# Decoding float64 weights on the chip: the magnitude moved from ScalarE to VectorE, the sign written as a 16-bit float, the weights held at 1/256 of their size

## Chip, cores and metric

The kernel runs on one core of one Trainium2 chip. The metric is the time of one execution on the device in microseconds, as the median of the runs. The engines are TensorE (PE, its weight loads PEld), VectorE (DVE), ScalarE (ACT), GpSimd (POOL) and SyncE (SP), whose queue issues most of the DMA transfers. Each engine runs its own instructions in the order in which they were put into its queue, and waits on semaphores for the others.

## What is computed

Attention that keeps only the 32 best keys of every query, and a feed-forward block with an ELU on its result.

```python
# q, k, v: (8, 8, 576, 64) float32;  w_in: (512, 2048), w_out: (2048, 512) float64
scores = scale * np.matmul(q, k.transpose(0, 1, 3, 2))
kth = np.partition(scores, -top_k, axis=-1)[..., -top_k:-top_k + 1]
scores = np.where(scores >= kth, scores, -1000000000.0)
attn = softmax(scores)                     # with 1e-09 added to the sum
x = (attn @ v) as (4608, 512)
h = x @ w_in
g = np.where(h > 0.0, h, np.exp(np.minimum(h, 0.0)) - 1.0)
out = (g @ w_out).astype(np.float32)
```

The two weight matrices arrive in float64. No engine computes in that format here, so the kernel reads them as pairs of 32-bit words and makes float32 numbers of them itself. That is the decoding, and the change is all about it.

## The kernel before

**Attention.** For each of the 8 batches the 576 queries are cut into four tiles of 128 rows and one of 64. One *step* is one tile with two heads (a row `i` = 0 or 1 for each head; the 64-row tile takes four heads in a step). A step multiplies queries and keys on TensorE (`scores`, L301), copies the scores to SBUF on ScalarE (L309), and finds the 32 largest of each row on VectorE: four `MAX8` passes with three `MATCH_REPLACE8` passes between them (`select_row` L320 to L330, later `select` L343 to L355). Then comes `mask`: GpSimd takes the negated 32nd value and the gap to the largest (L368, L370), ScalarE masks with a very steep Prelu (L371) and takes the exponential with its sum (L372). `normalise` (L382 to L389, GpSimd) divides, `turn` (L408, L409) transposes through TensorE and copies back on ScalarE, and `attend` (L434) multiplies with the values.

**Feed-forward.** `ffn_pieces` cuts the work into pieces. `hidden` multiplies with `w_in` (L506) and writes two Relus from PSUM (L516, L519) and an exponential (L521) on ScalarE; `close_gates` puts them together on VectorE (L478). `project` multiplies with `w_out` (L531), copies the result on ScalarE (L540) and stores it. `feed` deals these pieces out between the attention steps by a plan of costs and due steps (`HIDDEN`, `PROJECT`, `due`), so that TensorE has work all the time. A piece is only dealt out when the pieces of weights that it needs count as decoded (`decoded[0]`).

**Decoding.** The weights come in 32 pieces of 128 x 512 float64 numbers, 16 of each matrix, into a pool `raw` of seven buffers (`load_weight`, L153, SyncE). A number is two words, the low one (`lo`) and the high one (`hi`), so all operations of the decoding go over every second word. One call of `hook` runs `decode_piece(i)`: it issues the load of piece i + 3, the first half of the conversion of piece i (`convert_first`), and the second half for piece i - 3 (`convert_last`).

- L174, ScalarE: the top of the low word's mantissa becomes the low bits of a float32 (`Copy` with a scale and a bias).
- L175, ScalarE: the sign of the number, as an 8-bit float +1 or -1, into the top byte of the low word.
- L178, ScalarE: the magnitude of the high word, read as a float32, scaled by a power of two.
- L179, GpSimd: the magnitude is limited from both sides.
- L186, VectorE (three hooks later): the high word is shifted left by three, which turns the 11-bit exponent into an 8-bit one.
- L187, GpSimd: an integer addition of both words gives the float32 weight and adds the sign bit with the exponent's offset that comes with the sign's own exponent.

The hook is called in `select_row` after the third and the fourth `MAX8` of every row, that is four times in each of the first eight steps (`tight`), and three more times in `select`, where the later steps begin.

**What sets the order.** From step 8 on the program stands inside `manual_schedule`: the four compute engines execute what the Python program issues, in that order. In the first eight steps (apart from the very start) the planner of the language orders the instructions of each engine itself, with the order of the program as priority. The SyncE queue is in order throughout.

Of the kernel before, what the change touches and what calls it, by code (L numbers as in the profile page):

```python
# [8 lines left out]
AF = mybir.ActivationFunctionType  # L9
ALU = mybir.AluOpType  # L10
FP32 = mybir.dt.float32
U32 = mybir.dt.uint32
I32 = mybir.dt.int32
FP8 = mybir.dt.float8e4
PSUM = bass.MemoryType.PSUM

TOP_K = 32
# [2 lines left out]
STEEP = 1.0e30  # L20
HIDDEN = {1: 1.1, 2: 1.85, 3: 2.7}
PROJECT = 3.55


class Tile:
# [56 lines left out]
def kernel(  # L82
# [9 lines left out]
    nc = tc.nc  # L92
# [9 lines left out]
    NF = dff // P  # L102
# [3 lines left out]
    scale = 1.0 / float(D) ** 0.5  # L106
# [33 lines left out]
    raw = {}  # L140
# [10 lines left out]
    def load_weight(i):  # L151
        t = rawpool.tile([P, 2 * WN], U32, tag="raw", name="raw")
        nc.sync.dma_start(t[:], weight(i)[0])  # L153
        raw[i] = t

    def parts(t):
        words = t[:].rearrange("p (n w) -> p n w", w=2)
        signs = t[:].bitcast(FP8).rearrange("p (n w) -> p n w", w=8)
        return words[:, :, 0], words[:, :, 1], signs[:, :, 3]

    def convert_first(i):

        lo, hi, sign = parts(raw[i])
        ef, mf = hi.bitcast(FP32), lo.bitcast(FP32)
        nc.scalar.activation(mf, lo, AF.Copy, scale=2.0**-35, bias=2.0**17)  # L174
        nc.scalar.activation(  # L175
            sign, ef, AF.Sign, scale=2.0**64, bias=1.0, saturate=False
        )
        nc.scalar.activation(ef, ef, AF.Abs, scale=2.0**-62)  # L178
        nc.gpsimd.tensor_scalar(  # L179
            ef, ef, (2.0 - 2.0**-3 - 2.0**-23) * 2.0**-46, 2.0**-77, ALU.min, ALU.max  # L180
        )

    def convert_last(i):
        t, dst = raw.pop(i), weight(i)[1]
        lo, hi, sign = parts(t)
        nc.vector.tensor_single_scalar(hi, hi, 3, ALU.logical_shift_left)  # L186
        nc.gpsimd.tensor_tensor(  # L187
            dst.bitcast(I32), hi.bitcast(I32), lo.bitcast(I32), ALU.add
        )
# [15 lines left out]
    def decode_piece(i):  # L205
        if i < 2 * NF:
            if i + 3 < 2 * NF:
                load_weight(i + 3)
            convert_first(i)
        if i > 2:  # L210
            convert_last(i - 3)
            decoded[0] = i - 2
# [205 lines left out]
    def attend(g):  # L418
# [28 lines left out]
        while tiles:  # L447
            blk, lo, parts = tiles[0].block, tiles[0].cols.start, 0
            while tiles and tiles[0].block is blk:
                parts += 1  # L450
                hi = tiles.pop(0).cols.stop
            finish(blk, parts, g.hp, slice(lo, hi), ps[:, c0 : c0 + hi - lo])
            c0 += hi - lo
# [15 lines left out]
    def close_gates(keep=0, upto=None):  # L469

        while gates:
            put, group, dst, n = gates[0]
            if put > place[0] - keep if upto is None else group > upto:
                return
            gates.pop(0)
            nc.vector.scalar_tensor_tensor(  # L478
                out=dst, in0=n, scalar=-1.0, in1=dst, op0=ALU.add, op1=ALU.add
            )  # L480

    def ffn_pieces(blk):
        n_tok = blk.slots * P
        bank = dm // n_tok
        unit = max(2, bank)

        def hidden(f):
            if f == 0 and blk.number == 0:
                g = early.tile([P, NF, P], FP32, tag="g", name="gT")
                blk.gT = [g[:, 0:NG], g[:, NG:NF]]  # L490
            elif f % NG == 0 and blk.number > 0:
                g = late["g"].tile([P, NG, T], FP32, tag="g", name="gT")
                blk.gT.append(g[:])
            if f % unit == 0:
                if len(gates) > 1:
                    close_gates(upto=gates[0][1])
                if blk.number == 0:
                    n = earlyf.tile([P, 4 * P], FP32, tag="n", name="n")
                else:
                    n = late["f"].tile([P, 2 * T], FP32, tag="n", name="n")  # L500
                blk.n = n[:, 0 : unit * n_tok].rearrange("p (f t) -> p f t", f=unit)
            if f % bank == 0:
                ps = ps_f.tile([P, dm], FP32, tag="f", name="hps")
                blk.h = ps[:, 0 : bank * n_tok].rearrange("p (f t) -> p f t", f=bank)
            for i in range(NC):
                nc.tensor.matmul(  # L506
                    blk.h[:, f % bank, :],
                    w_in[:, i, f * P : (f + 1) * P],
                    blk.xT[:, i, 0:n_tok],
                    start=(i == 0),  # L510
                    stop=(i == NC - 1),
                )
            g, end = blk.gT[f // NG], f % NG + 1
            if end % bank == 0:
                n0 = f % unit + 1 - bank
                nc.scalar.activation(  # L516
                    blk.n[:, n0 : n0 + bank, :], blk.h, AF.Relu, scale=-1.0
                )
                nc.scalar.activation(g[:, end - bank : end, 0:n_tok], blk.h, AF.Relu)  # L519
            if end % unit == 0:  # L520
                nc.scalar.activation(blk.n, blk.n, AF.Exp, scale=-1.0)  # L521
                dst = g[:, end - unit : end, 0:n_tok]
                gates.append((place[0], (blk.number, f + 1 - unit), dst, blk.n))

        def project(s, part):
            close_gates(upto=(blk.number, (part + 1) * NF // 4 - 1))
            if part == 0:
                blk.o = ps_f.tile([P, dm], FP32, tag="f", name="ops")
            step = NF // 4
            for f in range(part * step, (part + 1) * step):  # L530
                nc.tensor.matmul(  # L531
                    blk.o[:],
                    blk.gT[f // NG][:, f % NG, s * P : (s + 1) * P],
                    w_out[:, f, :],
                    start=(f == 0),
                    stop=(f == NF - 1),
                )
            if part == 3:
                o = opool.tile([P, dm], FP32, tag="osb", name="osb")
                nc.scalar.copy(o[:], blk.o[:])  # L540
                for t in blk.tiles[s]:
                    p0 = t.cols.start - s * P
                    nc.sync.dma_start(out[t.rows, :], o[p0 : p0 + t.ql, :])

        part = HIDDEN[blk.slots]
        behind = 2 * NF if blk.number else 0
        return [
            (part, max(behind, NC * (f // 4 + 1)), lambda f=f: hidden(f))
            for f in range(NF)
        ] + [  # L550
            (PROJECT, max(behind, NF + (part + 1) * NF // 4),
             lambda s=s, part=part: project(s, part))
            for s in range(blk.slots)
            for part in range(4)
        ]
# [4 lines left out]
    for b in range(B):  # L560
        if b % 2 == 0:
# [5 lines left out]
            for part in division:  # L567
                blk = Block(len(blocks), len(part))
# [4 lines left out]
        for qt in range(J + 1):  # L573
# [8 lines left out]
            t = Tile(b, qt, rows, blk, slice(c0, c0 + n))  # L582
# [6 lines left out]
        for qts in order:  # L589
# [3 lines left out]
            for qt in qts:  # L593
                n = len(steps)
# [3 lines left out]
    for blk in sorted(blocks, key=lambda x: x.ready):  # L598
        due.append((blk.ready, total))
        total += NF * HIDDEN[blk.slots] + 4 * blk.slots * PROJECT  # L600

# [47 lines left out]
    for hp in range(1, NHP):  # L649
        load_v(0, hp)  # L650
    decode += [lambda i=i: decode_piece(i) for i in range(2 * NF + 3)]
    at(0, start_qk, 0, 2)
    at(1, start_qk, 0, 3)
# [93 lines left out]
```

## Time and profile before

| what | value |
|---|---|
| runs | 1667.3, 1667.61, 1669.78 us; median 1667.61 |
| profiled execution | 1667.86 us, its span 1666.1 us |
| busy over the span | PE 1598.7 (96%), DVE 1495.4 (90%), ACT 1164.9 (70%), POOL 630.4 (38%) |
| first and last decoding instruction | first L174 at 8.5 us, last L187 at 148.6 us |
| granted TensorE clock | 0.972 on average; 0.55 from 40 to 80 us, 0.67 from 80 to 120 us, 0.80 from 120 to 160 us, 1.00 from 160 us to 320 us |
| first selection pass on VectorE (L320) | 15.55 us |

In the views that follow, a line of the groups reads: line, engine, operation, written tile <- read tile, shape and type, count | busy us, mean ns of one | idle us of the engine just before them, and what ended the idle time. A line of the timeline begins with its start and its duration in us; the bracket at its end is the engine's idle time before it and who ended that. A line of the waits reads: who waited <- for whom: us in total, times, longest. A line of the stretches gives the length, then busy us and number of instructions of each engine, then the granted TensorE clock as a share of full speed, and DMA. A busy time contains everything between the start and the end of an instruction, also what it waits inside; back to back instructions of one engine overlap a little, so the distance of two starts is often less than a duration.

### The profile page before, as it was taken

Reading aid. Unit: us, or ns where it says so; the run is one execution under the profiler, and the core shown is the slowest. Engines: PE = TensorE matmul, PEld = TensorE weight load, DVE = VectorE, ACT = ScalarE, POOL = GpSimd, SP = SyncE. Lnnn points to the kernel's source line nnn. Section 1 sums busy time; section 2 is a strip of 40 time slices with the busy share of each in tenths; the row PEclk is TensorE's granted clock in tenths of the full one; section 3 lists DMA queues with packets and bytes.
Section 4 is the critical chain, followed back from the end, with each engine's and each line's share of the span. In section 5 each row is a group of like instructions: output and inputs, shape, how many; then the busy total and the mean of one; then the engine's idle time right before and its main releaser. Section 6 shows DMA issues by size and latency. Waiting matters only on the chain.

```text
span 1666.1 us, 26020 instructions
## 1 busy us (share of the span) xinstructions
PE 1598.7 (96%) x8560; PEld 1037.1 (62%) x8560; DVE 1495.4 (90%) x3044; ACT 1164.9 (70%) x2345; POOL 630.4 (38%) x1719
## 2 busy tenths in 40 slices
PE   5588999999999999999999999999999999999999
PEld 3365777657574767656566676755557575755565
DVE  5887999999999999999999999999999999998500
ACT  6997777668686767678667685868758585857521
POOL 2775444333334334333334333333333343332200
PEclk9568999999999999999999999999999999999999
DMA  7540111001100110011100111001200100000000
GB/s 212 169 145 7 23 48 31 7 15 44 48 1 7 44 42 22 1 28 37 42 14 1 49 29 35 1 14 43 50 13 1 28 15 29 7 7 7 7 14 13
DMA packets 101126, 56.21 MB, mean 34 GB/s; under 512 B 84096, under 2 KB 92288, under 8 KB 100992
## 3 DMA queue, kind: packets, MB, share of 16 engines
q1 hardware_dynamic: 99792, 54.26, 11.7%
q8 instruction: 68, 1.11, 0.3%
q14 instruction: 66, 0.54, 0.1%
q10 hardware_dynamic: 1200, 0.30, 0.1%
HBM read 45.09 MB, written 9.44 MB: 33 GB/s over the span
## 4 chain that ended last, share of the span: by engine, by line
PE 68%; DVE 21%; ACT 8%; issue 1%; POOL 1%; SPq 0%; DMA 0%; ACTq 0%; DVEq 0%; POOLq 0%
PE ops L531 25%; PE hps L506 21%; DVE wk L348 9%; PE avps L434 8%; DVE m L355 8%; PE scps L301 7%; PE eps L408 5%; DVE m L343 3%; ACT raw L175 1%; PE qkps L271 1%; DVE gT L478 1%; ACT sc L372 1%; ACT sc L371 1%; ACT et L409 1%; ACT raw L174 1%
## 5 line engine op out<-in xcount | busy, mean ns | idle before, releaser
L355 DVE MAX8 m<-wk 128x8 f32<-128x576 f32 x816 | 573.1, 741 | 0.0
L506 PE MATMUL hps<-xT,w_in 128*128 128x256 f32 (+2 forms) x2432 | 547.5, 374 | 0.1
L531 PE MATMUL ops<-w_out,gT 128*128 128x512 f32 x1152 | 523.4, 599 | 0.0
L506 PEld LDWEIGHTS hps<-xT,w_in 128*128 128x128 f32 x2432 | 405.8, 192 | 97.8 <-issue 24.8
L348 DVE MATCH_REPLACE8 wk<-m,wk 128x576 f32<-128x576 f32 x544 | 398.2, 737 | 0.0
L531 PEld LDWEIGHTS ops<-w_out,gT 128*128 128x128 f32 x1152 | 208.8, 190 | 233.5 <-issue 221.5
L382 POOL TENSOR_SCALAR dene<-den 128x2 f32<-128x2 f32 x144 | 36.4, 253 | 778.3 <-ACT sc L372 777.6
L371 ACT ACTIVATE sc<-sc,neg 128x576 f32<-128x576 f32 x288 | 226.3, 786 | 79.5 <-POOL neg L368 79.5
L372 ACT ACTIVATE sc<-sc,gap 128x576 f32<-128x576 f32 x288 | 223.8, 777 | 25.2
L301 PE MATMUL scps<-kqT 64*128 64x288 f32 (+1 forms) x1280 | 204.6, 443 | 27.9 <-ACT sc L309 15.6
L309 ACT ACTIVATE sc<-scps 128x576 f32<-128x576 f32 x288 | 173.6, 658 | 76.8 <-PE scps L301 76.8
L389 POOL TENSOR_SCALAR sc<-sc,rec 128x576 f32<-128x576 f32 x288 | 221.2, 778 | 14.9
L409 ACT COPY et<-eps 128x512 f32<-128x512 f32 x288 | 166.6, 578 | 58.1 <-PE eps L408 58.0
L408 PEld LDWEIGHTS eps<-ident,sc 128*128 128x128 f32 x1152 | 144.8, 145 | 88.0 <-issue 48.3
L348 DVE MATCH_REPLACE8 wk<-m,sc 128x576 f32<-128x576 f32 x272 | 199.1, 737 | 0.0
L434 PE MATMUL avps<-et,vT 128*64 128x256 f32 (+2 forms) x2080 | 193.3, 329 | 3.0 <-ACT et L409 2.7
L408 PE MATMUL eps<-ident,sc 128*128 128x128 f32 x1152 | 177.2, 280 | 19.2 <-POOL sc L389 17.9
L478 DVE SCALAR_TENSOR_TENSOR gT<-n,gT 128x512 f32<-128x512 f32 (+1 forms) x132 | 99.1, 751 | 103.1 <-ACT n L521 103.1
L343 DVE MAX8 m<-sc 128x8 f32<-128x576 f32 x272 | 190.5, 739 | 0.0
L301 PEld LDWEIGHTS scps<-kqT 64*128 64x128 f32 (+1 forms) x1280 | 109.0, 182 | 99.4 <-issue 44.9
L434 PEld LDWEIGHTS avps<-et,vT 128*64 128x64 f32 x2080 | 123.4, 142 | 76.2 <-issue 25.1
L516 ACT ACTIVATE n<-hps 128x512 f32<-128x512 f32 (+1 forms) x156 | 87.7, 562 | 72.6 <-PE hps L506 71.0
(46 smaller groups left out, 1160.3 us busy)
## 6 DMA issues: line engine op xcount, KB each, us to landing
kin<-in_k_dram SPq DMA_DIRECT2D x64, 128.0 KB, 2.9
raw<-in_moe_w_in_dram SPq DMA_DIRECT2D x16, 512.0 KB, 5.1
vT<-in_v_dram SPq DMA_DIRECT2D x64, 128.0 KB, 2.3
raw<-in_moe_w_out_dram SPq DMA_DIRECT2D x16, 512.0 KB, 3.9
out_dram<-osb SPq DMA_DIRECT2D x32, 256.0 KB, 2.3
qin<-in_q_dram SPq DMA_DIRECT2D x62, 128.0 KB, 2.8
kin<-in_k_dram SPq DMA_DIRECT2D x32, 32.0 KB, 2.6
vT<-in_v_dram SPq DMA_DIRECT2D x64, 16.0 KB, 2.2
```

Source lines behind the costliest of these rows:

```text
L301: nc.tensor.matmul(wide[i][rows, half, 0:HS], kq[part, q0 : q0 + u.t.ql], kq[part, k0 : k0 + HS], start=True, stop=True,)
L343: nc.vector.max(found[i], cur[i])
L348: nc.vector.match_replace(wk[i], found[i], cur[i], TAKEN)
L355: nc.vector.max(found[i], cur[i])
L371: nc.scalar.activation(sc, sc, AF.Prelu, bias=neg[:], alpha=STEEP)
L372: nc.scalar.activation(sc, sc, AF.Exp, bias=gap[:], accum_out=u.den[:, i : i + 1])
L389: nc.gpsimd.tensor_scalar(u.sc[:, i, :], u.sc[:, i, :], rec[:, i : i + 1], 1.0, ALU.mult, ALU.mult)
L408: nc.tensor.transpose(ps[:, c * P : (c + 1) * P], sc[:, c0 : c0 + P], ident[:])
L409: nc.scalar.copy(g.et[:, chunks, u.at, :], ps[:, 0 : n * P].rearrange("p (c q) -> p c q", c=n),)
L434: nc.tensor.matmul(ps[i * D : (i + 1) * D, cols], vt[:, 2 * J + i if c == J else i * J + c, :], w, start=(c == 0), stop=(c == J),)
L506: nc.tensor.matmul(blk.h[:, f % bank, :], w_in[:, i, f * P : (f + 1) * P], blk.xT[:, i, 0:n_tok], start=(i == 0), stop=(i == NC - 1),)
L531: nc.tensor.matmul(blk.o[:], blk.gT[f // NG][:, f % NG, s * P : (s + 1) * P], w_out[:, f, :], start=(f == 0), stop=(f == NF - 1),)
```

## The change

`convert_first` keeps the two ScalarE operations on the low word and on the sign. The sign is now written as a 16-bit float into the upper half of the low word. A new function, `convert_next`, runs one hook later: VectorE clears the sign bit of the high word with an AND, in place of the Abs on ScalarE, and GpSimd limits the magnitude, with other constants. A 16-bit float +1 has other exponent bits in that place than an 8-bit one, by eight steps of the weight's exponent, so the decoded weights are the true ones times 2 to the minus 8; the scales of the Relus that read the first product and of the output copy undo that.

```diff
-FP8 = mybir.dt.float8e4
+FP16 = mybir.dt.float16
...
+WEIGHT = 2.0**-8
...
     def parts(t):
         words = t[:].rearrange("p (n w) -> p n w", w=2)
-        signs = t[:].bitcast(FP8).rearrange("p (n w) -> p n w", w=8)
-        return words[:, :, 0], words[:, :, 1], signs[:, :, 3]
+        signs = t[:].bitcast(FP16).rearrange("p (n w) -> p n w", w=4)
+        return words[:, :, 0], words[:, :, 1], signs[:, :, 1]
...
     def convert_first(i):
         lo, hi, sign = parts(raw[i])
-        ef, mf = hi.bitcast(FP32), lo.bitcast(FP32)
-        nc.scalar.activation(mf, lo, AF.Copy, scale=2.0**-35, bias=2.0**17)
         nc.scalar.activation(
-            sign, ef, AF.Sign, scale=2.0**64, bias=1.0, saturate=False
+            lo.bitcast(FP32), lo, AF.Copy, scale=2.0**-35, bias=2.0**17
         )
-        nc.scalar.activation(ef, ef, AF.Abs, scale=2.0**-62)
+        nc.scalar.activation(
+            sign, hi.bitcast(FP32), AF.Sign, scale=2.0**64, bias=1.0
+        )
+
+    def convert_next(i):
+        hi = parts(raw[i])[1]
+        nc.vector.tensor_single_scalar(hi, hi, 0x7FFFFFFF, ALU.bitwise_and)
         nc.gpsimd.tensor_scalar(
-            ef, ef, (2.0 - 2.0**-3 - 2.0**-23) * 2.0**-46, 2.0**-77, ALU.min, ALU.max
+            hi.bitcast(FP32), hi.bitcast(FP32),
+            (2.0 - 2.0**-3 - 2.0**-23) * 2.0**17, 2.0**-14, ALU.min, ALU.max,
         )
...
             convert_first(i)
+        if 0 < i <= 2 * NF:
+            convert_next(i - 1)
         if i > 2:
             convert_last(i - 3)
             decoded[0] = i - 2
...
                 nc.scalar.activation(
-                    blk.n[:, n0 : n0 + bank, :], blk.h, AF.Relu, scale=-1.0
+                    blk.n[:, n0 : n0 + bank, :], blk.h, AF.Relu, scale=-1.0 / WEIGHT
                 )
-                nc.scalar.activation(g[:, end - bank : end, 0:n_tok], blk.h, AF.Relu)
+                nc.scalar.activation(
+                    g[:, end - bank : end, 0:n_tok], blk.h, AF.Relu, scale=1.0 / WEIGHT
+                )
...
-                nc.scalar.copy(o[:], blk.o[:])
+                nc.scalar.activation(o[:], blk.o[:], AF.Copy, scale=1.0 / WEIGHT)
```

## The prediction

> **What bounds the kernel now.** I read the span in stretches first, then the busy time by operation, the waits of the early stretch, and the timeline of single instructions there. The profiled execution took 1667.86 us (span 1666.1), 0.25 above the median of the three runs, 1667.61; I sum on the profile and take the gain off the median. Columns of the stretches: PE, PEld, DVE, ACT and POOL busy, then clock, DMA share, GB/s.
>
> ```profile
> 38.00:142.00 104.00, 73.74 (x372) 54.50 (x372) 74.58 (x155) 102.27 (x172) 71.39 (x119) 0.63 0.42 133
> ...
> 160.00:800.00 640.00, 626.79 (x3770) 423.57 (x3767) 640.00 (x1310) 470.20 (x972) 247.79 (x714) 0.99 0.11 27
> 800.00:1666.00 866.00, 859.94 (x4269) 536.10 (x4268) 739.89 (x1496) 558.82 (x1143) 289.19 (x829) 1.00 0.07 19
> ```
>
> After 160 us VectorE has no idle time until 800, then TensorE has almost none, and the order is fixed by the program. So an edit to the decoding of weights, which is over by 149 us, moves the end by as much as it moves the start of that dense part: I pass every microsecond through, gain or loss. TensorE does not forbid it: in the early stretch it is busy 73.7 of 104 us, at a granted clock of 0.63. From 38 to 142 us ScalarE is full, 102.3 of 104. Of the decoding alone that stretch holds (DVE, ACT, POOL):
>
> ```profile
> 38.00:142.00 104.00, 12.28 (x27) 66.39 (x86) 48.56 (x53) 0.63 0.42 133
> ```
>
> Two thirds of ScalarE's stage is decoding. VectorE is idle for 104 - 74.6 = 29.4 us of it, and the waits between 37 and 142 us say for whom:
>
> ```profile
> DVE raw L186 <- POOL raw L179: 22.8, 18, 4.0
> ...
> POOL raw L179 <- ACT raw L178: 13.4, 6, 3.9
> ...
> DVE gT L478 <- ACT n L521: 6.0, 2, 3.4
> ```
>
> VectorE's shift waits for GpSimd's limits, which wait for ScalarE's magnitudes. That is a chain with ScalarE at its head.
>
> **What the change takes off ScalarE.** The groups by shape, then one pair of pieces on ScalarE in order of time:
>
> ```profile
> L175 ACT ACTIVATE raw<-raw 128x512 fp8e4<-128x512 f32 x32 | 40.9, 1394 | 0.1
> ...
> L178 ACT ACTIVATE raw<-raw 128x512 f32<-128x512 f32 x32 | 21.0, 714 | 0.1
> ...
> L174 ACT ACTIVATE raw<-raw 128x512 f32<-128x512 uint32 x32 | 20.9, 711 | 5.1 <-DMA raw<-in_moe_w_in_dram 5.1
> ```
>
> ```profile
> 74.65 1.25 ACT L174 ACTIVATE raw<-raw 128x512 f32<-128x512 uint32 x2
> 75.78 2.50 ACT L175 ACTIVATE raw<-raw 128x512 fp8e4<-128x512 f32 x2
> 77.99 1.28 ACT L178 ACTIVATE raw<-raw 128x512 f32<-128x512 f32 x2
> 79.15 0.79 ACT L371 ACTIVATE sc<-sc,neg 128x576 f32<-128x576 f32 x1
> ```
>
> By the starts a piece costs 0.565 (Copy), 1.105 (Sign) and 0.58 us (Abs). Abs goes: 0.58. The sign with 16-bit output is in no row: it lies between 0.565, like the 4-byte outputs beside it in the same strided tile, and 1.105 as now. Less than 0.565 I exclude, since no pass over 512 elements here is cheaper by more than a few hundredths. I take 0.565: only the one-byte output is slow here, and the strides are the same. So 1.12 us a piece, and 29 of 32 pieces are converted after 38 us: 32.5 us, and ScalarE's load falls from 102.3 to 69.8.
>
> The page "ScalarE: Activation LUTs", section "What ACT_TABLE_LOAD costs", in the Trainium skill, gives every function one element per cycle, for fp32 and bf16 alike, with 186 ns + 0.833 ns an element. The sign row above breaks it at 1394 ns, so the rule as printed does not cover one-byte outputs; by it the new sign would last an estimated 613 ns, and the sum would be that of the forecast.
>
> **What it puts on VectorE.** One AND a piece, the form of the shift (uint32 words at the same stride, one constant). An unobstructed shift delays the next VectorE instruction by 0.41 us at most, so 29 x 0.41 = 11.9 us, and VectorE's load in this stage is 74.6 + 11.9 = 86.5. The stage can shorten by 104 - 86.5 = 17.5 us at the utmost. Two things come off that.
>
> First, VectorE and GpSimd block each other:
>
> ```profile
> 59.57 1.04 POOL L187 TENSOR_TENSOR w_in<-raw 128x512 int32<-128x512 int32 x1
> ```
>
> ```profile
> 59.62 1.27 DVE L186 TENSOR_SCALAR raw<-raw 128x512 uint32<-128x512 uint32 x1
> 60.82 0.75 DVE L330 MAX8 m<-wk 128x8 f32<-128x576 f32 x1
> ```
>
> This shift lasted 1.27 instead of 0.41: it ended 0.28 us after GpSimd's add did. Of the 32 shifts 20 had waited for data, mostly for GpSimd itself, and so met it idle or won against it (0.43 us each, the first 0.46). Of the other 12 three met it at work and lost 0.35, 0.86 and 0.35: on average 0.13 us. Once the shifts no longer wait, all 29 shifts and 29 ANDs are of this second kind: 58 x 0.13 = 7.5 us. The bounds are 0 and 58 x 0.52 = 30 (each loses the mean of those three); I take the mean over the 12, the nearest rows.
>
> The Trainium skill speaks here against the change: "SBUF — State Buffer", section "SBUF: two separate sides", says that a VectorE operation in a two-port mode and a GpSimd operation hold one port pair as an exclusive lock for a whole instruction. The row above agrees, but nine of the twelve free shifts were not held up; if all were by it, the sum would be that of the slower rival or worse.
>
> Second, new waits. The AND of piece i-1 stands at hook i in VectorE's in-order queue, ahead of the shift of i-3 and the next selection pass, and waits for ScalarE's Sign of i-1. The distance from conversion to first use on VectorE shrinks from three hooks to one. If Sign is late, the selection stands still, and with it GpSimd's negation and ScalarE's masking. GpSimd's limits go one hook later, past the add of the earlier piece and, for every second piece, past the row's negation and gap (in every second row the normalisation too). The loads on SP keep their places and are freed by the same adds. The price lies between 0 and today's 22.8 us. ScalarE's free time grows from 2% to nearly 30% of the stage, so I keep a fifth: 4.5 us.
>
> Before 38 us the first two pieces stand ahead of the first key copy and the first score copies on ScalarE; the second piece is tied to its load, which lands at 13.0 us, and its sign delays the score copy by 0.54 us less: 0.6 us gained, with bounds 0 and 1.3 (the first piece's Sign and Abs).
>
> **What costs nothing.** The hidden layer's Relu gets other constants: L516 with a scale and L519 without have 595 and 594 ns. The output copy becomes an ACTIVATE with a scale; against 578 ns for a 128x512 COPY from PSUM the ACTIVATE L516 has 595, so 36 x 0.017 = 0.6 us at most, behind 111.9 us of idle time before that line; uncovered, only the last copy's 0.02 us counts.
>
> Sum: 17.5 - 7.5 - 4.5 + 0.6 = 6.1 us. The median goes to 1661.5 us.
>
> **Rivals.** *GpSimd's hold (slower).* In the stage GpSimd is busy 71.4 of 104 us, and of fewer microseconds a larger part, some 0.72. If an AND or shift meets it that often and then loses the 0.52 us mean, the price is 0.72 x 0.52 x 58 = 21.7, and 17.5 - 21.7 - 4.5 + 0.6 = -8.1: 1675.7 us. It decides from (17.5 - 4.5 + 0.6) / 58 = 0.23 us an operation on. For it: the three long shifts, and that GpSimd runs the limits as soon as an AND ends, just when the shift is due. Against it: the nine free ones.
>
> *The sign stays slow (no change).* If 2-byte output is as slow as 1-byte, ScalarE loses only 29 x 0.58 = 16.8 and keeps 85.5 us beside VectorE's 86.5 + 7.5. Two full queues wait for each other more: I keep 40% of 22.8, 9.1, and no early gain. 104 - 94 - 9.1 leaves 0.9: 1666.7 us. For it: nothing in the trace shows a 2-byte output. Against it: the cause may as well be the 8-bit conversion, and I hold that likelier.
>
> *All of the slack is taken (faster still).* With no hold and no new wait 17.5 + 0.6 to 1.3: about 1649 us. It needs two engines without one wait between them.
>
> **How the numbers follow.** A measurement of this kernel tells some 0.2%, 3.3 us, from no change. Forecast 0.43, with its best end another 0.07: faster 0.50. Slow sign, or a forecast whose waits eat all but 3 us: same 0.20. GpSimd's hold, or late signs that act alike: slower 0.30. The order of the first eight steps is the planner's, not written by hand, so it can also change with the edit, in either direction; that keeps me from being surer. The range goes from 1650, a little inside the full slack, to 1677, a little beyond the slower rival; about 2 in 10 stay outside. The likeliest case alone spans 1655 to 1664.
>
> **What would show it.** Right: the sign near 0.7 us mean, no Abs, ScalarE near 70 us between 38 us and the stage's end, VectorE near full there, and its dense part starting about 6 us earlier. Wrong on the sign: still about 1.4 us. Wrong on the hold: ANDs and shifts with means over 0.64 us. Wrong on new waits: an AND that waits for Sign, more than 5 us in all. If the stage shortens and the end doesn't, the pass-through fails: idle time of VectorE between 160 and 800 us would show it.

## The result, and the profile after

The changed kernel takes 1674.3 us (median of six runs, 1671.97 to 1675.98) beside 1667.46 us of the kernel before in the same series. The ratio is 1.0036 with an interval of 1.0026 to 1.0047: slower by 6.8 us, where 6.1 us less had been forecast. The profiled execution took 1671.97 us, its span 1670.1 us. It is the quickest of the six, so the profile shows the loss a little too small.

The stretches, with the columns of the prediction:

```profile
38.00:142.00 104.00, 59.16 (x352) 43.41 (x350) 86.07 (x181) 89.20 (x143) 71.72 (x118) 0.72 0.44 135
160.00:800.00 640.00, 625.55 (x3774) 422.45 (x3773) 640.00 (x1305) 467.95 (x968) 249.09 (x719) 1.00 0.10 27
800.00:1666.00 866.00, 863.81 (x4284) 537.86 (x4282) 743.83 (x1506) 561.17 (x1150) 288.11 (x829) 1.00 0.07 19
```

Again VectorE is without a gap from 160 to 800 us and TensorE nearly so after that. The early stretch now has ScalarE at 89.2 of 104 us instead of 102.3, and VectorE at 86.1 instead of 74.6. Neither is full. The decoding alone (DVE, ACT, POOL), which was 12.28, 66.39 and 48.56:

```profile
38.00:142.00 104.00, 27.19 (x54) 54.53 (x58) 45.23 (x52) 0.72 0.44 135
```

ScalarE lost 12 us of decoding here and VectorE got 15. Beside the decoding VectorE did less in the same 104 us, 58.9 us of work instead of 62.3. The groups by shape, in the order of the answer, say why it is not more:

```profile
L177 ACT ACTIVATE raw<-raw 128x512 f16<-128x512 f32 x32 | 42.1, 1365 | 0.2
...
L183 DVE TENSOR_SCALAR raw<-raw 128x512 uint32<-128x512 uint32 x32 | 18.0, 563 | 26.5 <-ACT raw L177 26.4
...
L192 DVE TENSOR_SCALAR raw<-raw 128x512 uint32<-128x512 uint32 x32 | 14.8, 464 | 5.7 <-POOL raw L184 5.6
```

The first line is the sign: 1365 ns with a 16-bit output, 1394 with an 8-bit one. It did not get faster. L183 is the new AND, with 26.4 us of VectorE's idle time in front of it over the whole span, all of it for the sign. L192 is the shift. ScalarE's pair of pieces now, in order of time:

```profile
77.43 1.24 ACT L174 ACTIVATE raw<-raw 128x512 f32<-128x512 uint32 x2
78.55 2.52 ACT L177 ACTIVATE raw<-raw 128x512 f16<-128x512 f32 x2
80.80 0.75 ACT L379 ACTIVATE sc<-sc,neg 128x576 f32<-128x576 f32 x1
```

By the starts a sign costs (80.80 - 78.55) / 2 = 1.125 us. Abs is gone, the sign is as it was. The waits between 37 and 142 us:

```profile
DVE raw L183 <- ACT raw L177: 12.9, 11, 3.9
...
DVE raw L192 <- POOL raw L184: 4.9, 3, 3.0
```

Before, VectorE's shift had waited 22.8 us for GpSimd's limits. Now the AND waits 12.9 us for the sign and the shift 4.9 us for the limits. The longest of these waits, on all engines in order of time (a bracket holds the idle time before, and who ended it):

```profile
68.65 0.91 POOL L397 TENSOR_SCALAR sc<-sc,rec 128x576 f32<-128x576 f32 x1
...
70.12 0.27 ACT L417 COPY et<-scps 128x128 f32<-128x128 f32 x1 [0.67 <-PE scps L416]
...
71.45 1.22 ACT L174 ACTIVATE raw<-raw 128x512 f32<-128x512 uint32 x2
...
73.23 1.34 ACT L177 ACTIVATE raw<-raw 128x512 f16<-128x512 f32 x1
...
74.61 0.43 DVE L183 TENSOR_SCALAR raw<-raw 128x512 uint32<-128x512 uint32 x1 [3.94 <-ACT raw L177]
...
75.12 0.66 POOL L184 TENSOR_SCALAR raw<-raw 128x512 f32<-128x512 f32 x1 [2.35 <-DVE raw L183]
```

It goes round all engines. GpSimd normalises a row late (L397), after an add of the decoding. TensorE transposes that row late, ScalarE stands in front of the copy of it (L417), and then has the Copies of two pieces (L174) and a masking pass ahead of the first sign. VectorE stands 3.94 us at the AND with the next `MAX8` behind it, and GpSimd's limits (L184) stand 2.35 us for the AND.

The hold between VectorE and GpSimd is there too:

```profile
87.39 1.03 POOL L193 TENSOR_TENSOR w_in<-raw 128x512 int32<-128x512 int32 x1
87.47 1.25 DVE L183 TENSOR_SCALAR raw<-raw 128x512 uint32<-128x512 uint32 x1
```

This AND ended at 88.72, 0.30 us after GpSimd's add. Nine of the 32 ANDs lost time in this way, 4.6 us together, and six shifts 1.5 us.

### The profile page after: what moved, and what is told of

It reads as the page before. It is cut to its first block, busy times and chain, and to the rows that moved or that the text cites. A ratio compares the mean times of both kernels' runs of the same rounds, so it can differ in the third digit from the quotient of the medians.

```text
span 1670.1 us, 26030 instructions
## 1 busy us (share of the span) xinstructions
PE 1585.9 (95%) x8560; PEld 1026.6 (61%) x8560; DVE 1511.5 (91%) x3076; ACT 1148.3 (69%) x2313; POOL 631.0 (38%) x1719
## 4 chain that ended last, share of the span: by engine, by line
PE 69%; DVE 19%; ACT 7%; POOL 2%; issue 2%; SPq 0%; DMA 0%; ACTq 0%; POOLq 0%; DVEq 0%
PE ops L541 24%; PE hps L514 22%; DVE wk L356 8%; PE avps L442 8%; PE scps L309 7%; DVE m L363 7%; PE eps L416 5%; DVE m L351 2%; ACT sc L380 1%; PE qkps L279 1%; ACT sc L379 1%; DVE gT L486 1%; ACT raw L177 1%; PE scps L416 1%; ACT et L417 1%
## 5 line engine op out<-in xcount | busy, mean ns | idle before, releaser
L379 ACT ACTIVATE sc<-sc,neg 128x576 f32<-128x576 f32 x288 | 225.7, 784 | 89.6 <-POOL neg L376 89.5
L397 POOL TENSOR_SCALAR sc<-sc,rec 128x576 f32<-128x576 f32 x288 | 221.5, 779 | 15.0
L309 PE MATMUL scps<-kqT 64*128 64x288 f32 (+1 forms) x1280 | 199.9, 437 | 16.0 <-ACT et L417 5.6
L417 ACT COPY et<-eps 128x512 f32<-128x512 f32 x288 | 166.0, 576 | 62.3 <-PE eps L416 62.3
L442 PE MATMUL avps<-et,vT 128*64 128x256 f32 (+2 forms) x2080 | 189.1, 323 | 4.7 <-ACT et L417 4.5
L442 PEld LDWEIGHTS avps<-et,vT 128*64 128x64 f32 x2080 | 120.0, 139 | 77.4 <-issue 23.9
L309 PEld LDWEIGHTS scps<-kqT 64*128 64x128 f32 (+1 forms) x1280 | 106.6, 180 | 86.1 <-issue 45.4
```

Of the source, the lines that this page charges most:

```text
L309: nc.tensor.matmul(wide[i][rows, half, 0:HS], kq[part, q0 : q0 + u.t.ql], kq[part, k0 : k0 + HS], start=True, stop=True,)
L379: nc.scalar.activation(sc, sc, AF.Prelu, bias=neg[:], alpha=STEEP)
L397: nc.gpsimd.tensor_scalar(u.sc[:, i, :], u.sc[:, i, :], rec[:, i : i + 1], 1.0, ALU.mult, ALU.mult)
L417: nc.scalar.copy(g.et[:, chunks, u.at, :], ps[:, 0 : n * P].rearrange("p (c q) -> p c q", c=n),)
L442: nc.tensor.matmul(ps[i * D : (i + 1) * D, cols], vt[:, 2 * J + i if c == J else i * J + c, :], w, start=(c == 0), stop=(c == J),)
```

## The experiments

Every edit is to the changed kernel. Times are medians; "against before" is the difference to the median of the kernel before in the same series (1668.15, 1668.22 and 1668.08 us in the three series). "Stage" is how much later or earlier than in the kernel before VectorE's selection passes come at the end of step 8 (from 148 us of the kernel before on), in the profiles; "idle" is VectorE's idle time from 38 us to its last shift.

| run | against before, us | ratio and its interval | stage, us | idle, us |
|---|---|---|---|---|
| before | 0 | 1 | 0 | 29.4 |
| the change | +6.8 | 1.0036 (1.0026 to 1.0047) | +3.1 | 17.9 |
| sign16 | +0.7 | 1.0001 (0.9992 to 1.001) | +1.3 | 29.4 |
| and8 | +5.9 | 1.0031 (1.002 to 1.0043) | +6.0 | 21.5 |
| sign32 | -1.7 | 0.999 (0.9981 to 0.9999) | -3.1 | 12.9 |
| nolimits | -14.2 | 0.9916 (0.9903 to 0.993) | -14.0 | 13.1 |
| and_nolim | +1.5 | 1.0008 (0.9998 to 1.0017) | +2.1 | 17.0 |
| and_twice | +14.9 | 1.0086 (1.0073 to 1.01) | +15.3 | 16.7 |
| lag2 | +5.4 | 1.0031 (1.0021 to 1.004) | +4.5 | 17.3 |
| lag2sign32 | -4.8 | 0.9973 (0.9964 to 0.9982) | -4.9 | 9.3 |
| sign32abs | -4.8 | 0.9967 (0.9955 to 0.998) | -5.8 | 22.3 |
| nolow | -12.7 | 0.9923 (0.991 to 0.9935) | -13.9 | 15.3 |
| lean | -16.4 | 0.9894 (0.9881 to 0.9908) | -20.2 | 6.9 |

**Why is the sign slow?** The first run appends ScalarE operations to the end of the kernel, four of each form, all 128 x 512.

```diff
+    bench(halves[:, :, 1], bhi, AF.Sign, **big)
+    bench(quarters[:, :, 3], bhi, AF.Sign, saturate=False, **big)
+    bench(blo, bhi, AF.Sign, **big)
...
+    bench(flat16, flat, AF.Sign, **big)
+    bench(halves[:, :, 1], bhi, AF.Copy)
...
```

> The changed kernel with 56 more ScalarE operations behind its end, four each of fourteen forms over 128x512 elements, on scratch data; its time is longer by these and says nothing. Asked is why the sign takes 1.36 us with 16-bit output. If the narrow output is slow: Sign to dense or strided float32 near 0.7 us, Sign and Copy to the 16-bit and 8-bit places near 1.36. If the write into part of a word is slow: dense 16-bit output near 0.7, strided 1.36. If the function Sign is slow: every Sign near 1.3, Copy and Abs to the same places near 0.7, and Tanh either.

ScalarE's timeline; a line holds the four operations of one form:

```profile
1670.63 5.42 ACT L739 ACTIVATE bench<-bench 128x512 f16<-128x512 f32 x4
...
1676.08 5.43 ACT L739 ACTIVATE bench<-bench 128x512 fp8e4<-128x512 f32 x4
...
1681.55 2.70 ACT L739 ACTIVATE bench<-bench 128x512 f32<-128x512 f32 x4
...
1689.30 2.60 ACT L739 ACTIVATE bench<-bench 128x512 f16<-128x512 f32 x4
```

In order: sign to strided 16 bits, to strided 8 bits, to strided 32 bits, to dense 16 bits. One operation lasts 1335, 1335, 651 and 629 ns. Copy and Tanh with the strided 16-bit output have 1335 as well, Copy to strided 8 bits too, and Copy and Abs to strided 32 bits 651. So neither the function nor the conversion is slow, nor the stride alone, nor 16 bits alone: it is an output narrower than four bytes written with gaps. All the slow rows also read with gaps; a narrow output with gaps from a dense input, and other gaps, were not measured.

The same question inside the kernel: the sign as a 32-bit float over the whole low word. That overwrites what Copy wrote, so the three lowest bits of the weights are lost, but Copy stays for its time.

```diff
-WEIGHT = 2.0**-8
+WEIGHT = 2.0**-1
...
-        return words[:, :, 0], words[:, :, 1], signs[:, :, 1]
+        return words[:, :, 0], words[:, :, 1], words[:, :, 0].bitcast(FP32)
```

> The changed kernel with the sign written as a 32-bit float over the whole low word (weights at one half), so that it takes some 0.65 instead of 1.36 us; the three low bits from the low word are overwritten, and its conversion is kept only for its time. This is what the prediction assumed of the sign. Theory S: the forecast holds, 1658 to 1665, and VectorE waits for the sign less than 6 us. Theory W: the distance of one hook costs all the same, 1668 to 1675, with 10 us of wait or more.

Measured: 1666.52 us in eleven runs, 8.5 us better than the change by the differences to before. The sign's group, and the waits between 37 and 142 us (the line numbers are one lower than in the changed kernel):

```profile
L176 ACT ACTIVATE raw<-raw 128x512 f32<-128x512 f32 x32 | 21.0, 676 | 0.2
```

```profile
DVE raw L182 <- ACT raw L176: 7.5, 4, 3.3
...
DVE raw L191 <- POOL raw L183: 5.9, 3, 3.5
```

With the sign that the forecast had assumed the change is about even, and not 6 us faster: VectorE still idles 12.9 us. That lies between the two expectations: the quick sign is worth a good part of what was missing, and most of the waits stay with it.

**Which half of the change costs?** One keeps the 16-bit sign and the scales, and leaves the magnitude to an Abs on ScalarE, in its old place:

```diff
+        ef = hi.bitcast(FP32)
+        nc.scalar.activation(ef, ef, AF.Abs)
...
-        nc.vector.tensor_single_scalar(hi, hi, 0x7FFFFFFF, ALU.bitwise_and)
...
-            convert_next(i - 1)
```

> The changed kernel with the magnitude back on ScalarE (Abs), in convert_first ahead of GpSimd's limits; 16-bit sign and scaled weights stay. Theory 1 (the loss is the AND on VectorE: its time, the holds against GpSimd and the waits for the sign): as before within 2 us, since the sign costs 1.36 for 1.39 us: 1665 to 1670. Theory 2 (the loss comes with the 16-bit sign and the scales in the later operations): 1671 to 1676, near the changed kernel.

The other keeps the AND, with the 8-bit sign of before:

```diff
-WEIGHT = 2.0**-8
+WEIGHT = 2.0**-16
...
-        signs = t[:].bitcast(FP16).rearrange("p (n w) -> p n w", w=4)
+        signs = t[:].bitcast(FP8).rearrange("p (n w) -> p n w", w=8)
```

> The changed kernel with the sign as an 8-bit float again (weights then held at 2 to the minus 16); the AND on VectorE stays. Theory 1: like the changed kernel, 1671 to 1676, with VectorE waiting some 13 us for the sign. Theory 2: like before, 1665 to 1670.

The sign alone: 1668.86 us, no difference, and its waits between 37 and 142 us are those of before:

```profile
DVE raw L189 <- POOL raw L182: 23.4, 18, 4.0
...
POOL raw L182 <- ACT raw L181: 13.8, 6, 4.1
```

The AND with the limits behind it: 1674.01 us, the whole loss but for 0.9 us, which the intervals do not tell from nothing. So the 16-bit sign, the Relus' constants and the scaled output copy cost nothing together, and the loss is that of the magnitudes on VectorE.

**What does the AND cost, and what the limits behind it?** Three steps. First without AND and without GpSimd's limits; the shift drops the sign bit by itself, and only weights outside the limits, zero among them, come out differently.

```diff
-        nc.vector.tensor_single_scalar(hi, hi, 0x7FFFFFFF, ALU.bitwise_and)
-        nc.gpsimd.tensor_scalar(
...
-            convert_next(i - 1)
```

> The changed kernel without AND and without GpSimd's limits, so that numbers out of float32's range are no longer clamped; the shift drops the sign bit anyway. ScalarE keeps 2 of 3 operations. Theory 1: with no AND the waits of VectorE on the sign go (the shift follows three hooks later), ScalarE's stage falls by 29 x 0.58 = 17 us and GpSimd's by 29 x 0.65 = 19: faster than before by 8 to 17 us, 1650 to 1660. Theory 2: the gain is less, 1658 to 1668, by the later loss.

Then the AND, still without the limits:

```diff
         nc.vector.tensor_single_scalar(hi, hi, 0x7FFFFFFF, ALU.bitwise_and)
-        nc.gpsimd.tensor_scalar(
...
```

> The changed kernel without GpSimd's limits (numbers out of float32's range are no longer clamped); the AND stays one hook behind the sign. Beside nolimits it shows the AND alone, beside the changed kernel GpSimd's part. Theory P (GpSimd's queue is in the circle: its limits wait for the AND, its later work is late, ScalarE's masking waits for it, the next sign comes late): VectorE's wait for the sign falls from 13 us to under 7, 1660 to 1667. Theory N (the AND waits because ScalarE is full with the slow sign): the wait stays over 10 us, 1668 to 1673.

And the change with every AND issued twice:

```diff
         nc.vector.tensor_single_scalar(hi, hi, 0x7FFFFFFF, ALU.bitwise_and)
+        nc.vector.tensor_single_scalar(hi, hi, 0x7FFFFFFF, ALU.bitwise_and)
```

> The changed kernel with each AND issued twice in a row; the second changes nothing. If VectorE's time in the stage is the price, 32 more ANDs cost 32 x 0.36 = 12 us and up to 5 us of holds against GpSimd: 1684 to 1691. If the waits for the sign and the limits have room for them, less than half of that: 1674 to 1680.

Against before they are -14.2, +1.5 and +14.9 us. The AND alone thus takes 15.7 us with its holds and waits, the limits put behind it 5.3 more (to the change's +6.8), and 32 further ANDs another 8.1 by the medians. Without the AND VectorE had 90.89 us of work in the stage's 104, more than it has in the changed kernel, because the stage moved on faster (columns as above):

```profile
38.00:142.00 104.00, 84.17 (x417) 57.79 (x416) 90.89 (x185) 93.53 (x158) 59.00 (x106) 0.74 0.42 135
```

In this stretch TensorE executed 417 matmuls, 352 in the changed kernel. The second AND waits for nothing but the first. At 0.35 us from start to start 32 of them are 11.2 us, before any hold, and 8.1 were lost; 1683.01 us lies between the two expectations. The waits took up some of it, but most of them stayed: VectorE still idles 16.7 us, beside 17.9 and, in a second profile of the changed kernel's instructions (shown below), 21.5. The two largest waits of the AND in the run without limits, between 37 and 142 us:

```profile
DVE raw L183 <- issue: 7.3, 2, 4.7
...
DVE raw L183 <- ACT raw L177: 6.3, 4, 4.1
```

The AND waits 18.4 us there in all, 17.0 of them after 38 us, so the expectation in which the wait for the sign stays is the one that came. 7.3 are put down to nothing and 4.8 to GpSimd, but every one of these waits ended 0.09 us after the sign of the same piece, as here:

```profile
70.71 1.33 ACT L177 ACTIVATE raw<-raw 128x512 f16<-128x512 f32 x1
...
72.14 0.43 DVE L183 TENSOR_SCALAR raw<-raw 128x512 uint32<-128x512 uint32 x1 [2.56 <-issue]
```

The runs of this kernel spread widely (1665.8 to 1672.6), so the split into 15.7 and 5.3 is good to a few microseconds only.

**Does distance help?** The AND two hooks after the sign instead of one:

```diff
-        if 0 < i <= 2 * NF:
-            convert_next(i - 1)
+        if 1 < i <= 2 * NF + 1:
+            convert_next(i - 2)
```

> The changed kernel with the AND and the limits two hooks after ScalarE's half instead of one; the shift stays at three, so it comes one hook after the limits. Theory W (the AND stands too close behind the sign): VectorE's wait for the sign falls from 13 us to under 5 and the time to 1664 to 1669, unless the shift's wait for the limits grows by as much. Theory S (the slow sign keeps ScalarE full, and whoever uses its result waits): the waits move but stay, 1670 to 1676.

```profile
DVE raw L192 <- POOL raw L184: 14.2, 9, 4.7
...
DVE raw L183 <- ACT raw L177: 3.3, 4, 1.7
```

1673.59 us. The wait for the sign fell from 12.9 to 3.3 us, and that for the limits rose from 4.9 to 14.2: the same idle time (17.3 us) at another instruction. Then the same edit with the 32-bit sign:

```diff
-            convert_next(i - 1)
+            convert_next(i - 2)
...
+        return words[:, :, 0], words[:, :, 1], words[:, :, 0].bitcast(FP32)
```

> sign32 (the sign over the whole low word, three low bits overwritten, the fast sign that was predicted) with AND and limits two hooks after ScalarE's half, as in lag2. If with a free ScalarE the distance of one hook still costs, VectorE's waits fall from 12.9 us to under 8 and the time to 1660 to 1664; if the waits only move from the sign to the limits as in lag2, 1665 to 1669.

1663.29 us in eleven runs, beside 1666.52 with one hook: here distance gives 3.1 us by the differences to before, and the idle time falls to 9.3, a little over the 8 that were expected.

**Is ScalarE the better place, and where is the floor?** The 32-bit sign with Abs on ScalarE and no AND:

```diff
-        return words[:, :, 0], words[:, :, 1], signs[:, :, 1]
+        return words[:, :, 0], words[:, :, 1], words[:, :, 0].bitcast(FP32)
...
+        ef = hi.bitcast(FP32)
+        nc.scalar.activation(ef, ef, AF.Abs)
...
-        nc.vector.tensor_single_scalar(hi, hi, 0x7FFFFFFF, ALU.bitwise_and)
```

> The sign as in sign32 (low bits overwritten), but the magnitude by Abs on ScalarE, as before; no AND on VectorE. ScalarE's load in the stage is 29 x 0.54 = 16 us below that of before, VectorE's as before. Both theories: faster than before, 1653 to 1661; if it is faster than sign32, moving the magnitude to VectorE loses also where the sign is fast.

The same without the Copy of the low word, which this sign overwrites in any case:

```diff
-        nc.scalar.activation(
-            lo.bitcast(FP32), lo, AF.Copy, scale=2.0**-35, bias=2.0**17
-        )
```

> As sign32abs, without the conversion of the low word, whose result is overwritten there: the three low bits of the weights are left out, and ScalarE has two operations a piece, 1.15 us. Its load in the stage falls to about 70 us, below VectorE's 75. If ScalarE was still what VectorE waits for in sign32abs, 1648 to 1655; if VectorE and GpSimd are the limit by then, no more than 2 us better than sign32abs.

And only the sign, the shift and the add: no Copy, no AND, no limits.

```diff
-            lo.bitcast(FP32), lo, AF.Copy, scale=2.0**-35, bias=2.0**17
...
-        nc.vector.tensor_single_scalar(hi, hi, 0x7FFFFFFF, ALU.bitwise_and)
-        nc.gpsimd.tensor_scalar(
...
-            convert_next(i - 1)
```

> A piece is Sign (over the whole low word), shift and add alone: without the conversion of the low word (three low bits of the weights are left out), without the magnitude and without the limits (numbers out of float32's range are not clamped). ScalarE's load in the stage falls to some 55 us and GpSimd's to some 52, so VectorE is left as the limit: of its 29 us of waits nearly all go, and the stage ends 20 to 27 us earlier than before: 1642 to 1649. If TensorE at its lower clock or the loads of the weights become the limit, 1649 to 1655.

They take 1663.44, 1655.5 and 1651.7 us; the first misses its expectation by 2.4 us, the second by 0.5, and the last fell into its second case. With the quick sign Abs on ScalarE is 3.1 us better than the AND on VectorE in the same series (1663.44 beside 1666.52); with the slow sign it was 5.2 better (sign16 beside and8). Taking one more pass of 0.57 us a piece off a ScalarE that has 89.6 us of work in the stage gives 7.9 us. The barest decoding shows where pass-through ends. Its passes come 20.2 us early at the end of step 8, and 16.2 us from 179 us on; between 142 and 160 us TensorE is the one without a gap and VectorE has 13.71 of 18 us:

```profile
142.00:160.00 18.00, 18.00 (x156) 14.97 (x155) 13.71 (x30) 14.37 (x30) 7.68 (x22) 1.00 0.05 16
```

Three kernels beat both of the case by over ten microseconds: nolimits, nolow and lean. Each decodes less than the full weight. One that keeps all of it and beats the kernel before was not found.

## Why the prediction was wrong

**The sign's term.** It was bounded by 0.565 and 1.105 us and set to 0.565, on the argument that only a one-byte output is slow. It measured 1.125, the far end. It stands in the sum only through ScalarE's load, which came to 89.2 us instead of 69.8, and so through the waits. With the 32-bit sign in its place the kernel is 8.5 us better, two thirds of the 6.1 + 6.8 us between forecast and result. What decides is in the rows of the appended operations: under four bytes with gaps. The rows of the kernel before could not tell this, but they held no 2-byte output at all, and both ends of the bound deserved the same weight.

**The new waits.** They were set to 4.5 us, a fifth of the 22.8 of before, because ScalarE would have nearly 30% free. VectorE's idle time measured 17.9, and 12.9 even with the quick sign, when ScalarE has 75.6 of 104 us of work and so the free time that the forecast counted on. This is the step that was wrong in any case. ScalarE's mean free time did not bear on it: the AND is due one hook after its sign, and in that time ScalarE runs two Copies and a masking pass ahead of the sign, or stands for a transpose that GpSimd's late row delays. The rival of the slow sign had the sign right and the loss in the right place, but not two full queues (neither is full), and it missed by the same term: 9.1 where 17.9 came, which is more than the 7.6 us between its 1666.7 and the result.

**The holds.** 7.5 us for all ANDs and shifts; they lost 4.6 and 1.5. The shifts had lost 1.6 before the change as well, so only the 4.6 are new. The mean over the free shifts was a good price, the mean over the three held ones was not: the rival that lived on it named 1675.7 us, close to the result, and for the wrong reason.

**The ANDs.** 0.41 us was an upper bound; by the starts of free ones it is 0.35, so 29 x 0.35 = 10.2 instead of 11.9. **The early part.** 0.6 us was to be gained; the first selection pass came at 15.64 us instead of 15.55, none, since the sign was not quicker; with the 32-bit sign it came at 14.74. **The edits at nothing** were at nothing, by sign16.

The same sum with what was measured: 29.4 - 17.9 idle, less 10.2 and 4.6, is -3.3 us. The passes of step 8 are 3.1 us late. For the 32-bit sign: 29.4 - 12.9 - 10.2 - 4.1 (3.9 for the ANDs, 0.2 more for the shifts) = +2.2; its passes are 3.1 us early, and the medians show 1.7. So the form of the sum holds to about a microsecond, and the term of the new waits is the failed step: 4.5 forecast, 17.9 measured, of which 12.9 are left with the sign that was assumed. The holds and the ANDs were priced too high and hid some of it.

**Pass-through** was right to about a microsecond. In the changed kernel the delay is 3.1 us at the start of the dense part, 3.3 at 209 us, 3.7 at 361, 4.2 at 564 and 4.1 at the end; without AND and limits the lead of 14.0 becomes 14.5. It was not exact everywhere: the 2.1 us of and_nolim become 4.1 at the end, and the lead of sign32abs falls from 5.8 to 4.4, for which no cause was looked for. In lean 4 us of the lead are gone by 179 us, where TensorE has no gap.

**From one execution to the next.** The median of the change lost 6.8 us, its profiled execution 4.1. The profile of forms tells why: up to the appended operations TensorE, VectorE and ScalarE execute the same instructions in the same order as in the changed kernel. There the passes of step 8 are 6.7 us late, and VectorE idles 21.5 us instead of 17.9:

```profile
DVE raw L183 <- ACT raw L177: 16.2, 11, 3.9
...
DVE raw L192 <- POOL raw L184: 5.2, 3, 3.0
```

Most of the difference lies in two waits of the AND, 0.76 and 0.72 us in the change's own profile, 2.74 and 1.74 here. Ahead of the first, TensorE runs the same 36 matmuls of `hidden`; the first line is from the change's profile, the others are from forms:

```profile
94.35 4.29 PE L514 MATMUL hps<-xT,w_in 128*128 128x128 f32 x36
```

```profile
95.52 6.10 PE L514 MATMUL hps<-xT,w_in 128*128 128x128 f32 x36
...
100.54 0.60 ACT L524 ACTIVATE n<-hps 128x512 f32<-128x512 f32 x1 [2.28 <-PE hps L514]
...
105.28 0.45 DVE L183 TENSOR_SCALAR raw<-raw 128x512 uint32<-128x512 uint32 x1 [2.74 <-ACT raw L177]
```

The granted clock was 1.00 over the 4.29 us and 0.69 over the 6.10 us. ScalarE stands 2.28 us for the product, 0.23 in the change's profile, and the sign behind its Relu comes late by about as much. Ahead of the other wait 20 matmuls of `attend` take 1.31 us at a clock of 1.00 in the one and 2.40 us at 0.50 in the other, and there ScalarE stands 0.92 us for them. So TensorE and its clock are in the circle too.

**Open.** What sets the granted clock in each execution was not looked for, and whether dividing the pieces between ScalarE and VectorE would help was not tried.

## What to carry to other kernels

Idle time of an in-order engine is not room for new work as long as the engine's next instruction waits for others: price the new operation in full, and its own wait from what its producer has queued between two neighbouring hooks, not from the producer's mean load. Moving work from a full engine to one with gaps lost time here, where the gaps were waits for the full one in a circle; taking a ScalarE pass away altogether gave 7.9 us for 32 x 0.57 = 18.2 us of it. Where a term rests on a form of an operation that no row shows, both ends of its bound are live, and a few operations at the end of a kernel settle it.

## What was not expected of the hardware

A ScalarE pass over 128 x 512 that writes less than four bytes per element with gaps lasts 1335 ns, with 8 and with 16 bits, for Sign, Copy and Tanh; with four bytes and the same gaps 651 ns, and dense with 16 bits 629 ns.

The Trainium skill's page "ScalarE: Activation LUTs", section "What ACT_TABLE_LOAD costs", gives one element per cycle for fp32 and bf16 alike, and 186 ns + 0.833 ns an element for an operation with constant scale and bias, from which an estimate is 186 + 0.833 x 512 = 613 ns. The dense rows agree within 16 ns; the narrow ones with gaps take over twice that.

The hold of VectorE by GpSimd came in 9 of 32 ANDs and 6 of 32 shifts, though GpSimd was busy 72 of 104 us.

By the skill's page "SBUF — State Buffer", section "SBUF: two separate sides", a VectorE operation in a two-port mode and a GpSimd operation take one port pair as a lock for a whole instruction. The AND that ended 0.30 us after GpSimd's add agrees with it; that the AND is in such a mode is not shown by itself, and how seldom the hold happened was for the trace to tell.
